# A kernel of polysketch attention and a SiLU layer: every engine's order fixed by a plan, four column tiles in turn, first chunk transposed by PE

## The chip, the cores and the metric

One core of one Trainium2 chip. The metric is the device time of one execution in microseconds (us), as the median of several executions. The kernel before takes 137.73 us (3 executions, 137.29 to 138.01). The span of a profile runs from the first recorded instruction to the last. It is about 1.8 us shorter than the time of the same execution (135.7 against 137.52 for the kernel before).

In the profile, PE is TensorE, PEld its weight loads, DVE is VectorE, ACT is ScalarE, POOL is GpSimd and SP is SyncE. "L239" is a line of the kernel that ran. The chain of waits is followed back from the last instruction. Its lines give start, length, engine, tile and line; "x16" means 16 records run together.

## The reference, cut to what matters

```python
batch, n_heads, seq, head_dim, r = 4, 4, 1088, 32, 8
def phi(x):                       # 64 products of two 8-wide sketches
    a = einsum('rd,bhsd->bhsr', S1, x);  b = einsum('rd,bhsd->bhsr', S2, x)
    return einsum('bhsi,bhsj->bhsij', a, b).reshape(..., 64)
q_p, k_p = phi(q), phi(k)
kv = einsum('bhsf,bhsd->bhfd', k_p, v);  z = sum(k_p, axis=2)
attn = einsum('bhsf,bhfd->bhsd', q_p, kv) / (einsum('bhsf,bhf->bhs', q_p, z) + 1e-6)
x = attn.transpose(0, 2, 1, 3).reshape(4352, 128)
h = x @ w_in                      # 128 -> 2048
out = (h * sigmoid(h)) @ w_out    # SiLU, 2048 -> 128
```

There are four chunks (one for each batch entry) of 1088 rows. In the kernel each chunk gives two blocks of 512 rows for the layer, and the last 64 rows of all four chunks make a ninth block of 256. A block of 512 rows needs eight SiLUs of 128x1024 elements, so there are 64 big ones, and eight half ones for the ninth block.

## The kernel before

Projections run in float32 on 128x32 column tiles of PE (`tile_position`). The pool allocator and the order of the program text decide what each engine does next. The parts that matter here (cuts marked):

```python
def project(srcT, weights):              # keys: 2 weights, queries: 3
    ...
    for c in range(4):
        for i, w in enumerate(weights):  # A, B (, WM) one after the other in tile c
            dst = pa[32*c: 32*(c+1), i, :] if i < 2 else pb[32*c: 32*(c+1), 0:256]
            nc.tensor.matmul(dst, w, srcT[:, c, 0:256], start=True, stop=True,
                             tile_position=(0, 32 * c))
    for c in range(4):
        for i, w in enumerate(weights):  # the 32 columns that are left
            nc.tensor.matmul(...)
    ... # DVE transposes back

def k_side(b):
    nc.vector.transpose(out=KT..., in_=Kx[b]...)    # waits for the load of K
    ab = project(KT, [A, B])
    ... # outer products kp on DVE, key sums z (PE), WM (DVE), kv (PE), KV (DVE)

def q_side(b):
    ... # transposes, project(QT, [A, B, WM]), row scalars, three outer products qp
        nc.sync.dma_start_transpose(qt, qp...)      # then num on PE, copy to xT on ACT

def attn(b):
    if b + 1 < B:
        load_x(Kx, k, b + 1, "Kx"); load_v(b + 1); load_x(Qx, q, b + 1, "Qx")
    k_side(b); q_side(b)

attn(0)
for b in range(B):
    if b + 1 < B: attn(b + 1)
    for g in range(2): moe(xT[b][:, g, :], 512, store_main(b, g))
moe(xR..., B * XN, store_rest)                     # the ninth block, eight stores on one queue
```

The names in the traces: KT and QT are the transposed keys and queries, kp and qp their outer products, z the key sums and kv the sums of kp times v. WAB holds the weights of both sketches, and WM, made from z, those of the denominator. num is qp times kv, which gives xT, the input of the layer; qt is qp transposed. h is the layer's first product, g its SiLU and o the second product. PSUM is the memory that PE writes to, in banks. The prediction calls the layer MoE.

## Time and profile before

| what | us | view |
|---|---|---|
| first SiLU starts | 36.8 | timeline of ACT |
| 64 big and 8 half SiLUs, start to end | 36.8 to 128.5 | the same |
| after the last SiLU | 7.2 | chain of waits, span |
| busy share PE / ACT / DVE | 72% / 53% / 42% | first part of the page |

The page of the kernel before: busy time and share of each engine, then groups of instructions (operation, count, busy time, mean ns, idle time just before them and what ended it).

```profile
PE 97.1 (72%) x773; PEld 48.2 (35%) x784; DVE 56.9 (42%) x128; ACT 72.1 (53%) x90; POOL 15.4 (11%) x35
...
L239 ACT ACTIVATE g<-h_ps 128x1024 bf16<-128x1024 f32 (+1 forms) x72 | 65.6, 986 | 22.2 <-PE h_ps L237 10.6
...
L140 PE MATMUL pa<-KT_131,WAB 128*32 128x256 f32 x32 | 3.0, 509 | 15.6 <-DVE WAB L118 15.6
...
L158 DVE STREAM_TRANSPOSE KT_132<-Kx 128x1024 f32<-128x1024 f32 x2 | 2.5, 1240 | 5.1 <-DMA Kx<-in_k_dram 5.1
```

No engine is full over the whole span, so the shares alone say little. The idle times point to the start: PE stood 15.6 us until the weights (WAB) were on chip, although DVE had only a few small copies to make for them. The chain of waits of the kernel before tells why:

```profile
5.21 8.43 DMA Kx<-in_k_dram
...
13.66 0.04 DVE KT_132 L158
...
15.32 0.18 DVE WAB L118
...
15.63 2.01 PE pa L140 x16
...
31.80 3.18 DMA qt<-qp
```

DVE had the transpose of the second chunk's keys ahead of the WAB copies, and waited for that load until 13.66 us. The whole first chunk then went through before the first SiLU at 36.8 us. Once SiLUs run, PE's work for the next chunk interrupts them. This is the chain of waits of the kernel before in the warm stretch, where one chunk's key projections and sums, and later its query projections, are on PE:

```profile
60.45 1.01 PE pa L140 x16
61.46 0.15 PE pb L144 x14
61.61 0.97 PE h_ps L237 x4
62.58 0.80 PE z_ps L172 x18
...
66.70 1.01 PE pa L140 x6
...
69.50 0.52 PE pb L144 x6
70.11 1.03 ACT g L239
```

A pair of layer matmuls of 512 columns takes 0.43 us when nothing is in its way, so the four at 61.61 would take 0.86 and took 0.11 more. Both key sets together cost PE 1.01 + 0.15 + 0.11 = 1.27 us. The three query sets cost about 3.1 us (66.7 to 69.85), and ACT then waited for PE.

### The profile page before, as it was taken

The page shows a single profiled execution, that of the slowest core. Times are in us where ns is not written, and L with a number is a line of the kernel's source. Part 1 is how long each engine was busy: PE and PEld are TensorE (multiplying, and loading weights), DVE is VectorE, ACT ScalarE, POOL GpSimd, SP SyncE. Part 2 cuts the span into 40 slices and gives each one's busy share as a digit, 9 for nine tenths or more (in the row PEclk, how much of TensorE's full clock was granted, in tenths as well). Part 3 has the DMA queues.
Part 4 walks back from the last instruction along what each step waited for, and adds up shares of the span by engine and source line. Part 5 has one row for each costly group of instructions (what it writes and reads, how often), then busy time and mean ns, then how long its engine had stood idle before and what let it go on. Part 6 is the DMA issues. An engine that isn't in the chain of part 4 may idle for free.

```text
span 135.7 us, 2047 instructions
## 1 busy us (share of the span) xinstructions
PE 97.1 (72%) x773; PEld 48.2 (35%) x784; DVE 56.9 (42%) x128; ACT 72.1 (53%) x90; POOL 15.4 (11%) x35
## 2 busy tenths in 40 slices
PE   0000369500799997999999699999979999998800
PEld 0000256200255643335654234456333334345500
DVE  1250987893058489028269300944950020202010
ACT  0300000000557078988536995461979999998800
POOL 6990001700000900000000000000000000000000
PEclk9999999965589999999999999999999999999975
DMA  4999999906200612824000761220066131130411
GB/s 112 295 180 283 355 252 296 101 5 131 42 0 5 76 6 39 174 39 77 5 0 5 129 107 17 34 44 5 0 127 107 17 56 21 27 55 0 77 22 19
DMA packets 34569, 11.34 MB, mean 84 GB/s; under 512 B 31360, under 2 KB 33408, under 8 KB 34560
## 3 DMA queue, kind: packets, MB, share of 16 engines
q1 hardware_dynamic: 28800, 9.05, 28.9%
q0 software_dynamic: 5664, 2.16, 13.8%
q8 instruction: 6, 0.10, 0.3%
q10 hardware_dynamic: 96, 0.01, 0.1%
q14 instruction: 3, 0.02, 0.1%
HBM read 8.79 MB, written 2.23 MB: 81 GB/s over the span
## 4 chain that ended last, share of the span: by engine, by line
PE 55%; DMA 14%; ACT 13%; DVE 9%; issue 4%; ACTq 0%
PE h_ps L237 17%; PE o_ps L243 16%; ACT g L239 13%; DMA Kx<-in_k_dram 9%; PE pa L140 9%; DMA qt<-qp 5%; PE kv_ps L186 3%; PE pb L140 2%; PE pb L144 2%; PE num L225 2%; DVE qp L216 2%; DVE kp L167 2%; PE z_ps L172 2%; DVE proj L149 1%; DVE QT_133 L196 1%
## 5 line engine op out<-in xcount | busy, mean ns | idle before, releaser
L239 ACT ACTIVATE g<-h_ps 128x1024 bf16<-128x1024 f32 (+1 forms) x72 | 65.6, 986 | 22.2 <-PE h_ps L237 10.6
L243 PE MATMUL o_ps<-g,w_out 128*128 128x512 bf16 (+1 forms) x140 | 38.0, 367 | 0.5 <-ACT g L239 0.3
L237 PEld LDWEIGHTS <-w_in 128*128 128x128 bf16 x144 | 12.9, 97 | 20.1 <-issue 11.1
L246 DVE STREAM_TRANSPOSE ot<-o_ps 128x512 f32<-128x512 f32 (+1 forms) x9 | 6.1, 681 | 32.1 <-PE o_ps L243 26.9
L243 PEld LDWEIGHTS <-w_out 128*128 128x128 bf16 x144 | 13.6, 97 | 15.8 <-issue 2.7
L149 DVE STREAM_TRANSPOSE proj<-pa 128x256 f32<-128x256 f32 x16 | 6.2, 429 | 25.3 <-PE pa L140 18.4
L140 PE MATMUL pa<-KT_131,WAB 128*32 128x256 f32 x32 | 3.0, 509 | 15.6 <-DVE WAB L118 15.6
L77 POOL DMA_DIRECT2D Vb<-in_v_dram x16 | 8.7, 554 | 31.5 <-PE kv_ps L186 29.6
L225 PE MATMUL num<-qt,KV 128*64 128x512 bf16 (+1 forms) x24 | 4.4, 381 | 9.6 <-DMA qt<-qp 9.4
L216 DVE TENSOR_TENSOR qp<-aqs,proj 128x1024 bf16<-128x1024 f32 (+1 forms) x12 | 10.8, 954 | 0.1
L167 DVE TENSOR_TENSOR kp<-proj 128x1280 bf16<-128x1280 f32 (+1 forms) x8 | 10.3, 1332 | 0.0
L237 PE MATMUL h_ps<-xT_141,w_in 128*128 128x512 bf16 x29 | 9.2, 380 | 1.5 <-ACT g L239 1.0
L237 PE MATMUL h_ps<-xT_139,w_in 128*128 128x512 bf16 x30 | 9.0, 387 | 1.4 <-ACT g L239 0.7
L237 PE MATMUL h_ps<-xT_142,w_in 128*128 128x512 bf16 x32 | 9.5, 377 | 0.6 <-ACT g L239 0.5
L237 PE MATMUL h_ps<-xT_140,w_in 128*128 128x512 bf16 x30 | 9.0, 380 | 1.1 <-ACT g L239 0.7
L229 ACT ACTIVATE xT_139<-num 128x512 bf16<-128x512 f32 x2 | 1.2, 597 | 15.1 <-PE num L225 15.1
L175 ACT ACTIVATE zt<-z_ps 32x32 f32<-32x32 f32 x4 | 0.7, 176 | 15.2 <-PE z_ps L172 15.2
L140 PEld LDWEIGHTS pa<-KT_131,WAB 128*32 128x32 f32 x32 | 1.2, 134 | 16.5 <-issue 16.0
L225 PEld LDWEIGHTS <-KV 128*64 128x64 bf16 x24 | 1.4, 112 | 13.9 <-issue 11.1
L140 PE MATMUL pa<-QT_134,WAB 128*32 128x256 f32 x32 | 4.9, 385 | 0.0
L158 DVE STREAM_TRANSPOSE KT_132<-Kx 128x1024 f32<-128x1024 f32 x2 | 2.5, 1240 | 5.1 <-DMA Kx<-in_k_dram 5.1
L172 PE MATMUL z_ps<-proj 128*32 128x32 f32 (+1 forms) x72 | 3.9, 209 | 0.8 <-DVE proj L149 0.8
(70 smaller groups left out, 95.5 us busy)
## 6 DMA issues: line engine op xcount, KB each, us to landing
Kx<-in_k_dram SPq DMA_DIRECT2D x4, 544.0 KB, 6.1
Qx<-in_q_dram SPq DMA_DIRECT2D x4, 544.0 KB, 5.3
out_dram<-ot SPq DMA_DIRECT2D x32, 64.0 KB, 2.0
Vb<-in_v_dram POOLq DMA_DIRECT2D x16, 64.0 KB, 4.4
w_in<-in_moe_w_in_dram POOLq DMA_DIRECT2D x1, 512.0 KB, 8.8
w_out<-in_moe_w_out_dram POOLq DMA_DIRECT2D x1, 512.0 KB, 18.5
qt<-qp SPq DMA_TRANSPOSE x12, 3.2
Vx<-in_v_dram POOLq DMA_DIRECT2D x8, 8.0 KB, 3.1
```

The source lines that it names most:

```text
L77: nc.gpsimd.dma_start(t[32 * c: 32 * (c + 1)].rearrange("p h a d -> p h (a d)"), AP(tensor=v.tensor, offset=v[b, 0].offset + c * NB * D, a ...
L140: nc.tensor.matmul(dst, w, srcT[:, c, 0:256], start=True, stop=True, tile_position=(0, 32 * c))
L149: nc.vector.transpose(out=o[:, i, 0:NB, :].rearrange("p a r -> p (a r)"), in_=pa[:, i, :])
L167: nc.vector.tensor_tensor(out=kp[:, H * lo: H * hi], in0=_bc(a, 2, R), in1=_bc(bb, 1, R), op=ALU.mult)
L172: nc.tensor.matmul(z_ps[:HR, 0:HR], ab[:n, 1, t, :], ab[:n, 0, t, :], start=(t == 0), stop=(t == NB))
L186: nc.tensor.matmul(kv_ps[:, 64 * hp: 64 * (hp + 1)], kpf[:n, t, 128 * hp: 128 * (hp + 1)], vv, start=(t == 0), stop=(t == NB))
L216: nc.vector.tensor_tensor(out=qp, in0=_bc(aqs[:, H * lo: H * hi], 2, R), in1=_bc(bq[:, H * lo: H * hi], 1, R), op=ALU.mult)
L225: nc.tensor.matmul(num[64 * hp: 64 * (hp + 1), :n], KV[:, hp].rearrange("p h d -> p (h d)"), rhs, start=True, stop=True, tile_position=(0, ...
L237: nc.tensor.matmul(h_ps[:, jj, :n], w_in[:, j * P: (j + 1) * P], x, start=True, stop=True)
L239: nc.scalar.activation(out=g[:, :, :n], in_=h_ps[:, :, :n], func=ACT.Silu)
L243: nc.tensor.matmul(o_ps[:, :n], w_out[:, j, :], gs[j // 2][:, j % 2, :n], start=(j == 0), stop=(j == NJ - 1))
L246: nc.vector.transpose(out=ot[:, :n], in_=o_ps[:, :n])
```

## The change: intent and diff

The intent is to start the layer earlier, to make attention cheaper on PE, and to place what is left so that no engine waits. A `Plan` simulates all engines with a guessed cost of each task, sorts by due times, and fixes every engine's order. Projections and key sums run "four column tiles in turn". The first chunk's first half goes through eight PE transposes and two copies on ACT instead of a DMA transpose. The last stores go out on three queues. The core of the diff (cuts marked):

```diff
+class Plan:                       # greedy: the earliest possible task; a due one may go ahead of it
+    def run(self, stretch=1.3):
+        ...
-        for c in range(4):
-            for i, w in enumerate(weights):
-                nc.tensor.matmul(dst, w, srcT[:, c, 0:256], ..., tile_position=(0, 32 * c))
+    def mm_set(dst, srcT, w, lo, hi):         # one weight, four tiles in turn, 288 columns
+        for c in range(4):
+            nc.tensor.matmul(dst[32*c: 32*(c+1), lo:hi], w, srcT[:, c, lo:hi],
+                             start=True, stop=True, tile_position=(0, 32 * c))
...
+        pr = [pl.add("PE", 0.55, lambda sl, i=i: proj(i, sl), st["kt"], take=pool) for i in range(2)]
...
+            if pe:                            # chunk 0, first half
+                e = pl.add("PE", 0.4, ... pet(lo, hi, f, sl), [o], take="o")
+                c.append(pl.add("ACT", 0.55, ... petc(lo, hi, f), [e] + c, give=e))
+            else:
+                c = [pl.add("SP", 1.3 if n > 1 else 0.7, ... dmat(lo, hi), [o], lag=2.2)]
...
+    key_tasks(0, pool="h")
+    query_tasks(0, [(0, 4)], pool="h", pe=True, at=5.3)
+    query_tasks(0, [(4, 8), (8, 9)], at=6.0)  # its second half comes later
+    for b in range(1, B):
+        load(b); key_tasks(b); query_tasks(b, [(0, 4), (4, 8), (8, 9)])
```

## The prediction

> **What bounds it now.** Three stretches (timeline, chain of waits).
> (1) 0 to 36.8 us: no SiLU runs. The window table shows ScalarE 1.5 us busy in 0 to 17. The page's groups show PE idle 15.6 us until the WAB copies: VectorE ran in program order, stood 5.1 us at chunk 1's key transpose until its load landed (13.66), and the WAB copies, needed by chunk 0's first matmul, were queued behind it. Then chunk 0 goes through whole: projection 15.6, outer products until 31.8, DMA transpose 3.2, num, first h at 36.1.
> (2) 36.8 to 128.5: MoE, 91.7 us. Where undisturbed the period is 0.915 us per 1024-wide SiLU; PE needs about 0.87 (four 512-column matmuls), so both engines are nearly full. 64 x 0.915 + 8 half ones (4.0) = 62.6. Attention of chunks 1 to 3 occupies PE in between, about 7.4 us each, read at 60.4 to 69.7: key projection 1.3, key sums 0.85, L2 0.3, kv 0.95, query projection 3.1, num 0.9. That makes 22. About 7 us are stalls (3.25 for one DMA transpose at 76; a cold PE at 36 to 38.5).
> (3) 128.5 to 135.7: last o, transpose, eight stores issued one after another by one queue.
>
> **What the change does.**
> - Start. WAB before everything that waits for a load, chunk 1 loads last. K0 lands about 5.5 (before: 5.2), KT 6.9, keys projected cold about 8; on VectorE then transposes 1.1, kp 1.45, half-sized query work 2, qp 1.22: about 13.4. Eight PE transposes and two 0.6 copies replace the 3.2 us DMA. KV must wait for kp's second half (1.2) and two more query transposes, so it is ready about 15.8; num, copy, h: first SiLU at 17.7, 19 us earlier.
> - Column tiles. Before, consecutive matmuls often hit the same column tile. The Trainium skill ("TensorEngine Tiling (Array Packing)", Key Properties) says different tiles execute in parallel. The trace agrees: 16 key records of 256 columns took 1.09 us at 60.4, about 1.7 if serial (estimate, 256/512 of the 0.216 us pace). Four tiles in turn should give 0.5 for keys, 0.75 for queries, 0.35 for sums: 3.6 us less per chunk, 11 us in all. PE is the path while attention interrupts the MoE, so nearly all counts.
> - Order. Later DMA transposes are planned early enough; I expect one stall of 1 to 3 us near 18 to 22 (chunk 1's keys lie behind both weights on one queue) and 1 to 2 near 30, where chunk 0's second half comes back.
> - Clock. 16 same records took 1.95 us at 22.4 against 1.09 at 60.4. "TensorE: Matmul & The Clock Gate", Part 1, calls this a half-rate clock until PE has been busy some 3.4 us. The first MoE pairs will be cold again: about 2 us lost.
> - End. Eight stores on three queues: about 2 us less.
>
> **Sum.** 17.7 + 62.6 + 3 x 3.75 (attention left on PE) + 1.2 (second half of chunk 0) + 5.5 stalls = 98.2; tail 4.8; span 103, plus 1.8 (run minus span before): 104.5 us. Range 99 to 110. Faster 0.97, same 0.02, slower 0.01.
>
> **Shows it right or wrong.** First SiLU between 16 and 20; PE key projection records at a third to a half of their time in the warm stretch; ScalarE busy share near 70%; SiLU period 0.92 outside attention; no DMA transpose in the chain over 1 us; tail under 5.5.
>
> **What would make it wrong.** The weights or chunk 1 landing after 20 us, since seven loads now share the start; tiles that don't overlap (+8); fixed order making one late item hold an engine; VectorE late for chunk 0's second half (+4); PE cold for longer.

## The result, and the profile after

The kernel after takes **115.99 us** (median of 4; 115.12 to 117.98). Its ratio to the kernel before is 0.8416, with a 95% interval of 0.834 to 0.8491. Ratios here are the mean time of one kernel's runs over that of the other's of the same rounds, so they are not quite the ratio of the medians. The direction was right, but the time lies 6 us above the upper end of the range.

The page of the kernel after, first part:

```profile
PE 93.7 (82%) x647; PEld 39.9 (35%) x657; DVE 59.3 (52%) x117; ACT 73.7 (65%) x93; POOL 16.0 (14%) x38
```

PE is busy for 93.7 us, only 3.4 us less than before, where the prediction had counted on 11 less from the column tiles. That is the first sign of where the miss lies. The span, laid beside the prediction's sum (span 103.05, measured 113.7):

| term | predicted | measured | how it was measured | off |
|---|---|---|---|---|
| first SiLU | 17.7 | 20.58 | timeline of ACT | +2.9 |
| to the end of the stalls: the first 12 SiLUs, chunk 1's attention | 12 x 0.915 + 10.45 = 21.4 | 21.57 | 20.58 to 42.15 | +0.1 |
| the other 52 SiLUs, attention of chunks 2 and 3 | 47.6 + 7.5 = 55.1 | 60.3 | 42.15 to 102.43 | +5.2 |
| 8 half SiLUs | 4.0 | 5.6 | 102.43 to 108.03 | +1.6 |
| after the last SiLU | 4.8 | 5.7 | 108.03 to 113.7 | +0.9 |

The 10.45 are chunk 1's attention (3.75), chunk 0's second half (1.2) and the stalls allowed for (5.5). The 47.6 is 52 x 0.915.

The start, in the chain of waits of the kernel after. Compare it with the 15.63 and 31.80 of before:

```profile
1.32 3.58 DMA Kx<-in_k_dram
...
4.92 0.79 DVE KT_88 L241
...
13.73 1.22 DVE qp L369
14.95 1.15 DVE kp L258
...
16.15 0.95 PE A_145 L289 x8
...
17.78 0.57 PE H_141 L400
```

The second chunk's load no longer stands in the way, and the DMA transpose is gone from this part. The kv sums (L289, eight records of 64 columns) take 0.95 us, and 0.72 where the clock is full (the run e11_warm below).

The stall before chunk 0's second half, same view:

```profile
22.43 2.63 DVE kp L258 x2
25.05 1.16 DVE QT_91 L337
...
26.34 1.10 DVE qp L369
...
27.47 5.43 DMA qt<-qp
...
32.94 0.41 PE A_144 L400 x2
...
35.77 0.26 PE A_145 L400
36.04 0.98 PE H_140 L459 x2
...
37.10 1.03 ACT G_148 L463
```

The outer product of chunk 0's second half (qp at 26.34) was planned for 21.34. On DVE it came after chunk 1's key products (kp) and query transpose (QT_91). Its DMA transpose took 5.4 us; those of before took 3.2 (median). Then PE stood in front of the small num of the last 64 columns (35.77), which nobody needs before the ninth block, with the layer's next pair (36.04) behind it. That num waited for a second, small transpose, which took 6.9 us (DMA view, issued at 29 to 31 us). PE had stood idle for 1.32 us before the big num and 1.89 us before the small one, and the pair then ran at half the clock (0.98 us; 0.54 behind another small num, at 60.01, with a granted clock of 1.00, where it was 0.50 at 36 to 38 us). In the plan the first h stood at 15.41 (19.5 in the trace), and the second half's big num at 26.39 (32.94).

The warm stretch, same view (compare 60.45 to 61.61 of before):

```profile
66.25 0.43 PE H_140 L459 x2
66.69 0.62 PE A_145 L204 x8
67.31 0.54 PE H_141 L459 x2
...
70.73 0.44 PE A_145 L265 x18
```

One set (four matmuls, eight records) costs 0.62 us and 0.11 on the pair after it: 0.73 us. A chunk has five: 3.65 us. With the sums (0.44 + 0.11), the L2 product (0.14), kv (0.95), two num (0.45 each) and the small one (0.26) that makes 6.45 us of PE for a chunk. The prediction had 3.75. The difference, 2.7 us for each of chunks 2 and 3, is the 5.2 of the table within 0.2 us. PE was the path there: from 42.15 to 87.05 us it was busy for 44.36 of 44.90 us (window table).

The end, same view. The half SiLUs took 5.6 us:

```profile
106.71 0.38 PE O_142 L470 x2
107.09 0.23 PE H_141 L459 x2
...
107.41 0.61 ACT G_151 L463
...
108.06 0.39 PE O_142 L470 x2
```

In the ninth block the plan put the o matmuls ahead of the next h, so that ACT waits for o (0.38) and h (0.23) before every second SiLU. In the kernel before, seven of them ran without a gap in 3.97 us.

### The profile page after: what moved, and what is told of

Read it like the earlier page. It is cut to its first block, busy times and chain, and to the rows that moved or that the text cites. A ratio compares the mean times of both kernels' runs of the same rounds, so it can differ in the third digit from the quotient of the medians.

```text
span 113.7 us, 1788 instructions
## 1 busy us (share of the span) xinstructions
PE 93.7 (82%) x647; PEld 39.9 (35%) x657; DVE 59.3 (52%) x117; ACT 73.7 (65%) x93; POOL 16.0 (14%) x38
## 4 chain that ended last, share of the span: by engine, by line
PE 54%; ACT 16%; DVE 14%; DMA 8%; issue 3%; POOL 1%; POOLq 0%; SPq 0%; ACTq 0%
PE H_141 L459 10%; PE O_143 L470 9%; PE H_140 L459 9%; PE O_142 L470 8%; DMA qt<-qp 5%; PE A_145 L204 4%; DVE kp L258 3%; PE A_144 L204 3%; DMA Kx<-in_k_dram 3%; ACT G_148 L463 3%; DVE qp L369 3%; ACT G_149 L463 3%; ACT G_147 L463 3%; ACT G_150 L463 3%; PE A_145 L289 2%
## 5 line engine op out<-in xcount | busy, mean ns | idle before, releaser
L459 PEld LDWEIGHTS <-w_in 128*128 128x128 bf16 x144 | 12.4, 102 | 18.5 <-issue 11.1
L463 ACT ACTIVATE G_146<-H_140 128x1024 bf16<-128x1024 f32 (+1 forms) x12 | 12.0, 1000 | 3.1 <-PE A_144 L204 2.1
L463 ACT ACTIVATE G_151<-H_141 128x1024 bf16<-128x1024 f32 (+1 forms) x12 | 11.6, 965 | 3.4 <-PE H_141 L459 2.6
L463 ACT ACTIVATE G_148<-H_140 128x1024 bf16<-128x1024 f32 (+1 forms) x12 | 12.0, 996 | 2.5 <-PE H_140 L459 2.3
L463 ACT ACTIVATE G_147<-H_141 128x1024 bf16<-128x1024 f32 (+1 forms) x12 | 12.0, 996 | 2.1 <-PE H_141 L459 2.1
L463 ACT ACTIVATE G_149<-H_141 128x1024 bf16<-128x1024 f32 (+1 forms) x12 | 12.0, 999 | 1.5 <-PE H_141 L459 1.4
L463 ACT ACTIVATE G_150<-H_140 128x1024 bf16<-128x1024 f32 (+1 forms) x12 | 11.5, 959 | 2.1 <-PE A_145 L204 1.3
L446 POOL DMA_DIRECT2D out_dram<-ot x2 | 1.1, 560 | 80.2 <-DVE ot L475 80.2
L369 DVE TENSOR_TENSOR qp<-aqs,qabm 128x1024 bf16<-128x1024 f32 (+1 forms) x12 | 11.1, 939 | 0.1
L258 DVE TENSOR_TENSOR kp<-kab 128x1280 bf16<-128x1280 f32 (+1 forms) x8 | 10.6, 1350 | 0.1
L475 DVE STREAM_TRANSPOSE ot<-O_143 128x512 f32<-128x512 f32 x4 | 2.9, 718 | 13.7 <-PE O_143 L470 13.7
L475 DVE STREAM_TRANSPOSE ot<-O_142 128x512 f32<-128x512 f32 (+1 forms) x5 | 3.3, 664 | 12.7 <-PE O_142 L470 12.5
L253 DVE STREAM_TRANSPOSE kab<-A_145 128x288 f32<-128x288 f32 x3 | 1.4, 480 | 9.3 <-PE A_145 L204 9.3
L459 PE MATMUL H_140<-xT_135,w_in 128*128 128x512 bf16 x15 | 5.6, 457 | 0.3 <-ACT G_148 L463 0.3
L459 PE MATMUL H_141<-xT_135,w_in 128*128 128x512 bf16 x15 | 5.3, 433 | 0.2 <-issue 0.2
L459 PE MATMUL H_141<-xT_138,w_in 128*128 128x512 bf16 x16 | 4.8, 379 | 0.3 <-ACT G_151 L463 0.2
L459 PE MATMUL H_141<-xT_137,w_in 128*128 128x512 bf16 x16 | 4.8, 383 | 0.0
L459 PE MATMUL H_140<-xT_137,w_in 128*128 128x512 bf16 x15 | 4.6, 381 | 0.1
L459 PE MATMUL H_141<-xT_136,w_in 128*128 128x512 bf16 x15 | 4.6, 382 | 0.0
L289 PEld LDWEIGHTS <-kp 128*128 128x128 bf16 (+1 forms) x72 | 3.7, 103 | 2.1 <-issue 0.4
```

The source lines that it names most:

```text
L253: nc.vector.transpose(out=st["ab"][:, i].rearrange("p a r -> p (a r)"), in_=st[f"p{i}"][:, 0:CW])
L258: nc.vector.tensor_tensor(out=st["kp"][:, H * lo: H * hi], in0=_bc(a, 2, R), in1=_bc(bb, 1, R), op=ALU.mult)
L289: nc.tensor.matmul(st["kvp"][:, 64 * hp: 64 * (hp + 1)], kpf[:n, t, 128 * hp: 128 * (hp + 1)], Vb[b][:n, 2 * hp: 2 * hp + 2, t, :], start= ...
L369: nc.vector.tensor_tensor(out=qp, in0=_bc(st["aqs"][:, H * lo: H * hi], 2, R), in1=_bc(bq, 1, R), op=ALU.mult)
L446: eng[2 * r + c].dma_start(AP(tensor=out.tensor, offset=out[4 * NB + c, 32 * r].offset, ap=[[SA * DM, 32], [S * DM, B], [1, 32]]), o[32 * ...
L459: nc.tensor.matmul(cc[jp][:, jj, :n], w_in[:, j * P: (j + 1) * P], x, start=True, stop=True)
```

## The experiments

Each kernel is the kernel after with one edit. "Moves" are made on the plan's finished order, so that nothing else is planned anew, unless said otherwise. All results were correct.

### What a projection set costs

**e1_double.** Every set is issued twice.

```diff
-        for c in range(4):
+        for c in 2 * list(range(4)):
```

> Every projection set (four 288-column fp32 matmuls in four column tiles) is issued twice in a row into the same bank; the result stays right. Measure: in the stretch with a full clock (after 42 us), the time from the start of the matmul pair before a set to the start of the pair after it, less the 0.43 us of a pair. In the changed kernel that is 0.72 us. Theory D (the tiles do overlap; 0.24 us is streaming[...], and some 0.48 us is entering and leaving the column-tiled mode): 0.96 us. Rival S (the tiles overlap badly, the 0.72 us is the work itself): 1.2 to 1.4 us. Whole kernel: D about +4 to +5 us, S about +9 to +12 us.

Measured: 121.21 us (one execution). From the chain of waits:

```profile
69.84 1.18 PE A L204 x16
71.02 0.54 PE H L459 x2
```

Two sets cost 1.18 + 0.11 = 1.29 us here (and 1.22 at most other places of the same chain, where the record is 1.11). So the second set adds about 0.49 to 0.56, and about 0.24 is paid once. D's 0.96 failed. The cost of the two sets lies in S's range (1.2 to 1.4), but the kernel became 5.2 us longer, near D's 4 to 5. S's reading, that the tiles overlap badly, is settled by e17 and e18 below: they overlap fully, and one set is longer work than D took it for.

**e2_adjacent.** Each tile's 288 columns in two halves, both halves of a tile in a row, so that neighbours in the order hit the same tile.

```diff
+        mid = (lo + hi) // 2
         for c in range(4):
-            nc.tensor.matmul(dst[.., lo:hi], w, srcT[:, c, lo:hi], ...)
+            for l, u in ((lo, mid), (mid, hi)):
+                nc.tensor.matmul(dst[.., l:u], w, srcT[:, c, l:u], ...)
```

> Each tile's 288 columns are cut in two halves that are issued one after the other before the next tile's turn, as consecutive matmuls met the same tile in the kernel before. Same columns in all. Same measure as for e1_double (0.72 us in the changed kernel). Theory D (tiles overlap only with other tiles): five serial slots of 0.12 us instead of two, 0.60 + 0.48 = 1.08 us per set. Rival S (no useful overlap anyway): stays near 0.72 to 0.8 us.

Measured: 113.61 us (one execution); a set cost 0.74 us instead of 0.72 to 0.73, the number of rival S and not D's 1.08. Two neighbours on the same tile do no harm, which contradicts the ground on which the prediction expected a gain from taking the tiles in turn. Why the whole kernel was 2 us shorter was not followed up: only one execution was taken, and its trace differs from that of after mainly in the length of the stall.

**e17_same_tile and e18_two_tiles.** Each full set is followed by four more of the same matmul, all in tile 3, or in tiles 2 and 3.

```diff
-        for c in range(4):
+        for c in (0, 1, 2, 3) + ((3, 3, 3, 3) if hi - lo == CW else ()):   # e17
+        for c in (0, 1, 2, 3) + ((2, 3, 2, 3) if hi - lo == CW else ()):   # e18
```

> The after kernel, in which each full set (four 288-column matmuls in tiles 0 to 3) is followed by four more of the same matmul, all in tile 3 (same result). In e1_double four more in tiles 0 to 3 cost 0.49 us. Theory P2 (a float32 matmul streams its columns twice, 0.24 us for 288 columns on one tile at the 512-column pace of 0.216 us, and tiles overlap two at a time): the four more cost 0.96 us. Theory P4 (a float32 matmul takes four times its columns, 0.49 us on one tile, and four tiles do overlap fully): they cost 1.9 to 2.0 us. Theory P1 (the same rate on one tile as on four, no overlap at all): 0.49 us. Read in the warm stretch from the chain, set and following pair, not from the kernel's time (which should be 5 to 20 us longer than after).

> As e17_same_tile, with the four more in tiles 2, 3, 2, 3. P2 (two at a time is all there is): 0.49 us for the four more, as in e1_double. P4 (overlap grows with the number of tiles): 0.95 to 1.0 us. P1: 0.49 us.

Measured in the warm stretch: 143.94 and 128.15 us in all. Chain of waits of e17_same_tile:

```profile
65.28 2.56 PE A L204 x16
67.84 0.54 PE O L470 x2
```

and of e18_two_tiles:

```profile
63.26 1.59 PE A L204 x16
64.86 0.54 PE H L459 x2
```

The four more cost 2.56 - 0.62 = 1.94 us in one tile, 1.59 - 0.62 = 0.97 in two, and 0.49 in four (e1_double, e9_grouped). P4 is right and P1 and P2 are wrong. (Only the time of the whole kernel missed: e17 is 28 us longer than after, not 5 to 20.) A float32 matmul of 288 columns takes 1.94 / 4 = 0.485 us in its tile. That is four times its columns at the pace of the bf16 matmuls (0.216 us for 512). And four tiles do overlap fully. So 0.49 us is what a set costs with perfect overlap. The four extra matmuls of e17 also write the same columns of the same bank one after another. So does the second set of e1_double, at 0.49, but a version of e17 with separate columns was not run.

With this the sets of before can be judged (estimates from these numbers): eight matmuls of 288 columns, one by one, would take 8 x 0.485 = 3.9 us, and perfect overlap 0.97. They took 1.27, of which about 0.24 is the fixed part if it was the same there. The keys of before were then already within 0.1 us of perfect overlap, so there was nothing to win. The queries of before, with three matmuls in a row in each tile, took about 3.1 where perfect overlap takes 1.46. Why they overlapped less than the keys is not shown: e2 had two in a row, and no run had three.

**e9_grouped.** The two key sets are one task, and so are the three query sets (from chunk 0's second half on); the plan is made anew.

```diff
-        pr = [pl.add("PE", 0.55, lambda sl, i=i: proj(i, sl), st["kt"], take=pool) for i in range(2)]
+        pr = pl.add("PE", 1.2, proj, st["kt"], take=pool, need=2)       # both sets, two banks
...
+            pr = [pl.add("PE", 0.24 + 0.165 * nn, set3, [t, kst["wm"]], take=pool, need=need)]
```

> Projection sets are issued together: both key sets in one go, all three query sets in one go (from chunk 0's second half on), so the column-tiled mode is entered and left twice per chunk instead of five times; same columns. After e1 and e2 I put a set at 0.48 us of streaming plus 0.24 us of changing mode. Theory: the key group costs 1.20 us of PE (start of pair before to start of pair after, less 0.43) instead of 2 x 0.72, the query group 1.68 instead of 3 x 0.72: 0.7 us less per chunk, 2 us in all, if the plan's other moves do no harm (it makes a new order). Rival 1, no cost of changing mode (0.72 all streaming): 1.44 and 2.16. Rival 2, mode change 0.48 as in theory D: 0.96 and 1.2.

Measured: 111.66 us, ratio 0.8111 (0.8042 to 0.818). Chain of waits:

```profile
62.44 1.11 PE A L209 x16
63.55 0.54 PE H L502 x2
...
68.22 1.60 PE A L367 x32
69.82 0.54 PE O L513 x2
```

One, two and three sets cost 0.73, 1.22 and 1.71 us: 0.49 each and 0.24 once. That a part is paid once for each group is shown. That it is the change of tiling is a reading: 0.11 of it lies in the pair that follows, and the kv sums, which use no column tiles, leave the same 0.11 behind them (a pair of 0.54 at 82.94 us of after). The kernel's gain is not all due to it, as the stall at 27 to 37 us also changed with the new plan.

### The stall before chunk 0's second half

**e3_rest_late.** Moves the num and copy of chunk 0's last 64 columns to just before the next use of their PSUM bank.

```diff
+        nxt = next(e for e in order[at + 1:] if e[0]["take"] == "att" and e[0]["slot"] == m["slot"])
+        ... # m8 and x8 of chunk 0 are taken out and put in front of nxt
```

> In the changed kernel PE and ScalarE stood at chunk 0's last 64 columns (num from the second, small DMA transpose, 35.8 us) although nothing needs them before the end, with the h of the second half behind them in order. Here this num and its copy come just before the next use of their PSUM bank; nothing else moves. Theory order: the first h of the second half starts right after its copy, about 34.0 instead of 36.0 us, one cold pair less: 2 to 3 us less than the changed kernel (ratio to before about 0.82 to 0.827 against 0.842). Rival (another wait ends at the same time, as the outer products or key transposes of the next chunk on VectorE): under 0.7 us less.

Measured: 111.47 us, ratio 0.8123 (0.8066 to 0.8179). Chain of waits:

```profile
26.80 5.14 DMA qt<-qp
...
33.09 0.60 PE H L463 x2
...
33.77 1.03 ACT G L467
```

The layer's pair starts at 33.09 instead of 36.04, at the full clock, and five SiLUs follow without a gap. A small num at the wrong place of a fixed order cost some 4 us.

**e4_loads_late.** Moves chunk 3's loads (POOL) behind chunk 0's second half, held by a one-column copy on POOL that reads it.

```diff
+        order[at:at] = [(dict(fn=lambda: nc.gpsimd.tensor_copy(out=gate, in_=xT[0][:, 1, 0:1])), ())] + mine
```

> Chunk 3's loads (K, V, Q) wait, by a one-column copy on GpSimd, until chunk 0's second half is copied to xT; in the changed kernel they run from 20 to 35 us, over the DMA transposes of 27.5 us, of which the first landed after 5.4 us against 3.1 in the median. Theory contention: that transpose lands in about 3.2 us, PE's wait before num shrinks by 2 us and the small one follows, 2 to 4 us less in all. Rival (the transpose is slow for another reason, for instance two transposes issued together, or chunk 2's loads): it still takes over 4.5 us, time within 1 us of the changed kernel.

Measured: 111.84 us, ratio 0.8127 (0.8086 to 0.8168). The time gained what was expected, but not by the way that was expected. From issue to landing (DMA view), the big transpose of the second half took 4.6 us here and 5.4 in after, where 3.2 (the median of all twelve before) had been expected, and over 4.5 by the rival. The small one of the last 64 columns took 3.6 instead of 6.9, so that its num ran at 32.61 instead of 35.77. Hardly anything else moved at that time. The next big transpose, which now runs under the moved loads, took 5.21 us. So moving the loads took 0.8 us off the big transpose and 3.3 off the small one, the one that PE had stood for; why the big one still takes 4.6 stays unexplained.

**e5_both.** Both moves together.

> e3_rest_late and e4_loads_late together. They gave 0.8123 and 0.8127 of the kernel before, 0.029 less than the changed kernel each. Theory: both cure the same stall (PE and ScalarE waiting for chunk 0's second half, and the cold PE after it), so they do not add: 0.803 to 0.812. Rival, independent stalls: 0.78 to 0.79.

Measured: 112.44 us, ratio 0.817 (0.8105 to 0.8235). The gains do not add, as the theory said, though the ratio lies above its range too: both moves remove the same wait for the small num. What is left is the wait for the big transpose, 5.03 us in the chain even with the loads moved away, and the next one, now under the moved loads, took 4.89.

**e6_pe_second.** e3_rest_late, and chunk 0's second half goes through eight PE transposes and two ACT copies instead of the DMA.

```diff
+    def pet2():
+        for t in range(8):
+            nc.tensor.transpose(pt[:, t, :], qf[:, t, :], identb)
+        for f in range(2):
+            nc.scalar.activation(out=qt[:, 4*f: 4*f + 4], in_=pt[:, 4*f: 4*f + 4], func=ACT.Copy)
```

> e3_rest_late with chunk 0's second half transposed on PE (eight transposes, two copies of 0.6 us on ScalarE) instead of by the DMA, all other instructions in the same order. Theory: the DMA transpose's 5 us is the last wait there; without it the first h of the second half starts at 31.5 to 32.3 us instead of 33.1 in e3_rest_late, PE does not stand over 0.8 us before it, and the kernel is 0.5 to 1.5 us faster than e3_rest_late (ratio 0.80 to 0.809). Rival: the copies delay SiLU by what they save; equal to e3_rest_late within 0.5 us.

Measured: 110.99 us, ratio 0.8078 (0.7997 to 0.8158). The second half's first SiLU comes at 32.97 instead of 33.77, and the kernel gains 0.5 us, within the intervals of e3. The wait for the DMA is gone. The chain now runs through DVE's list until 24.25 us (chunk 1's kp), and from 24.30 through PE's own list, almost without a gap, to the num at 31.25.

**e8_dma_first.** Undoes one part of the change: chunk 0's first half by DMA transpose, planned anew.

```diff
-    query_tasks(0, [(0, 4)], pool="h", pe=True, at=5.3)
+    query_tasks(0, [(0, 4)], pool="h", at=5.3)
```

> One part of the change undone: chunk 0's first half goes through the DMA transpose again (the plan then makes its own order; qp is ready at 15 us, loads of chunk 1 and 2 are in flight). PE transposes took from 15.0 to 16.7 us and KV was only ready at 17.4, so PE transposes cannot have won more than the DMA's time beyond 17.4. If the DMA transpose takes 3.4 us as in the quiet kernel before, the first SiLU comes 1 to 1.5 us later than 20.6; if it takes over 5 us as under loads, 3 to 4 us later. I expect the second: first SiLU at 23.5 to 24.5, kernel 2 to 4 us slower than the changed one.

Measured: 114.21 us, ratio 0.8271 (0.8178 to 0.8363). The first SiLU came at 24.70, close to what was expected (its DMA transpose took 6.47 us), but the kernel was not slower than after: it was some 2 us faster, with intervals that just overlap (after: 0.834 to 0.8491). The expectation that an early start is worth its time was wrong: in after, ACT stands still later, because the second half is not ready, and in e8 it hardly does (the gap before it, at 36.47, is 1.25 us). The 4 us that the PE transposes gain at the start were given back in the stall.

**e12_measured.** The plan gets eighteen costs as the trace of after showed them (a set 0.7, kv 0.95, a transpose's lag 2.6 to 3.6, and so on), with the grouped sets of e9 and the last block's order of e10; planned anew. Chunk 0's second half still goes through the DMA transpose.

```diff
-            pl.add("PE", 0.15 + 0.045 * nn, lambda sl, i=i: proj(i, sl), ...)
+            pl.add("PE", 0.7, lambda sl, i=i: proj(i, sl), ...)
... # seventeen more of this kind
```

> e9_grouped with the half order of e10, and the plan's costs replaced by those measured in the changed kernel's trace (outer products 0.3 per block, projections 0.7, kv 0.95, query scalars 1.0 + 0.12 per block, the first DMA transposes 4.9 us with issue). Theory (the stall came from a plan whose clock runs ahead of the chip): chunk 0's qp of the second half is now before chunk 1's key work on VectorE, PE does not stand over 1 us between 25 and 40 us, and the kernel takes 106 to 109 us (ratio 0.77 to 0.79). Rival (order is not what was wrong): 110 us or more.

Measured: 117.8 us, ratio 0.85 (0.8438 to 0.8561), 6 us slower than e9_grouped, the same kernel without the new costs and the half order, and no faster than after (the intervals overlap). A miss. Chunk 0's second half did come early (its rows at 30.67). But the first SiLU slipped to 21.22, and later chunks arrive with nothing in hand. PE in the timeline of e12_measured, with idle time before a group in brackets:

```profile
84.75 0.59 PE L514 MATMUL O<-G,w_out 128*128 128x512 bf16 x2 [0.31 <-ACT G L507]
87.25 0.41 PE L432 MATMUL A<-qt,KV 128*64 128x512 bf16 x2 [1.91 <-DMA qt<-qp]
88.34 1.61 PE L503 MATMUL H<-xT,w_in 128*128 128x512 bf16 x4 [0.69 <-ACT xT L440]
```

PE runs dry for chunk 3's transpose and then works at half the clock (1.61 us for four matmuls that otherwise take 0.86). Better costs alone did not make a better plan. A likely reason, argued and not tested, is that a greedy plan that brings each chunk just in time has no slack when a transpose takes 3.2 us instead of the planned 2.6. Which of the eighteen costs did the harm was not separated.

### The cold clock at the start

**e11_warm.** Idle PE at the start is filled with matmuls of zeros into a free bank: nine before the first work, five behind chunk 0's first kv part.

```diff
+    def dummies(n):
+        for _ in range(n):
+            nc.tensor.matmul(bank("o", 1), dum[:, 0:P], dum[:, P:], start=True, stop=True)
+    dummies(9)
```

> Nine matmuls of zeros before chunk 0's first work and five in PE's idle time at 12.5 us keep PE busy; nothing else moves. Theory clock: the records of chunk 0 then run at full clock (a first h pair in 0.6 us instead of 1.0, num 0.41 instead of 0.63, kv's second half unchanged), and the first SiLU starts at 18.3 to 19.3 us instead of 20.6; kernel 1 to 2 us faster, if the later stall does not take it back. Rival (the start is set by VectorE, loads and hops, not by PE's clock): first SiLU within 0.5 us of 20.6.

Measured: 113.94 us, ratio 0.8248 (0.8197 to 0.83). The first SiLU came at 18.38 instead of 20.58: kv 0.72 us, the first h pair 0.60. The cold clock is worth 2.2 us of the 2.9 that the start was late. The stall before the second half grew meanwhile (its two DMA transposes took 6.6 and 7.1 us), and its first SiLU came at 35.47, against 37.10 in after.

### The order in the last block

**e10_half_order.** In the ninth block, each h goes ahead of the o of two before it.

```diff
+        for jp in range(NJ // 2 - 2):
+            ... # move h[jp + 2] in front of o[jp]
```

> One thing moved: in the last, half-wide block each h pair comes before the o pair that the plan had put in front of it (as the scheduler of the kernel before had it). In the changed kernel the eight half SiLUs took 5.6 us (102.43 to 108.03), two in 1.34 us, with o waiting for the newest SiLU in front of the next h; in the kernel before 4.0 us. Theory: 4.0 to 4.3 us again, 1.3 to 1.6 us less for the kernel. Rival (another wait sets the pace): under 0.5 us.

Measured: 114.05 us, ratio 0.8231 (0.8181 to 0.828). ACT in the timeline of e10_half_order:

```profile
98.97 3.56 ACT L468 ACTIVATE G<-H 128x1024 bf16<-128x1024 f32 x4
102.86 3.97 ACT L468 ACTIVATE G<-H 128x512 bf16<-128x512 f32 x7 [0.32 <-PE H L464]
```

Seven half SiLUs again run in 3.97 us, as in the kernel before. The span of the profile fell from 113.7 to 112.6.

### Together

**e13_combo.** e6_pe_second and e10_half_order.

> e6_pe_second plus the half order of e10, the plan's list otherwise untouched. If both gains are separate: 1.3 to 1.6 us less than e6_pe_second, 109.2 to 109.8 us (ratio 0.795 to 0.80).

Measured: 110.67 us, ratio 0.8003 (0.7955 to 0.805). That is less than e10 alone, but the interval overlaps that of e6 alone (0.7997 to 0.8158): of the 1.3 to 1.6 us expected on top of e6, the ratios show about 1 us, the medians 0.3.

**e14_combo_warm.** e13_combo with the dummies of e11_warm.

> e13_combo (110.67 us, ratio 0.8003) with the dummy matmuls of e11_warm at the start, nothing else moved. Theory A (the stall before chunk 0's second half was what took back the gain of the warm start in e11; e13 has hardly a stall there, so the gain now arrives at the end): first SiLU about 18.3 us (e13: near 20.4), second half of chunk 0 starts its SiLUs 1 to 2 us earlier than e13's 33.3 us, and the kernel takes 108.5 to 109.3 us, ratio 0.785 to 0.791. Rival B (between 22 and 33 us VectorE's list for chunk 1 and 0 sets when the second half is ready, whatever happens before): first SiLU 18.3 us too, but the second half's first SiLU within 0.5 us of 33.3 and the kernel at 110 to 110.7 us, ratio 0.796 to 0.801.

Measured: **109.77 us**, ratio 0.7918 (0.7884 to 0.7952), the fastest of all. But the test is not clean. The first SiLU was expected at 18.3 and came at 19.57. ScalarE in the timeline of e14_combo_warm:

```profile
17.38 0.60 ACT L417 ACTIVATE xT<-H 128x512 bf16<-128x512 f32 x1 [1.70 <-PE H L409]
19.57 1.02 ACT L474 ACTIVATE G<-H 128x1024 bf16<-128x1024 f32 x1 [1.59 <-PE H L470]
```

In this profile the clock fell in spite of the dummies: the window table has a granted clock of 0.79 at 15 to 17 us and 0.50 at 17 to 19, and the first h pair took 1.03 us. So only 0.4 us was gained at the start here, and 0.57 at the second half (32.72 against 33.29). The ratio is 0.0085 below that of e13, about 1.2 us of the time before, and their intervals just fail to touch. Even that leans on two of the six executions (110.38 and 110.86) left out as slow, being over 1.5% above the fastest. Whether a start that stays warm would pass on its full 2 us stays open. Theory A's first step did not happen, and B was not tested.

**e15_combo_grouped and e16_grouped_warm.** e9_grouped with the three other parts of e13_combo, without and with the dummies.

> e9_grouped (projection sets of a chunk issued one after the other, so PE changes its tiling fewer times) with the three other parts of e13_combo (chunk 0's last 64 columns late, its second half by PE transposes, h in front of o in the last block). If a change of tiling costs 0.24 us of PE and two less per 5 sets are saved for keys and queries together 0.24 + 2 x 0.24 = 0.7 us per chunk in the PE-bound stretch (chunks 2 and 3, and part of chunk 1): 1.4 to 2 us under e13, 108.6 to 109.3 us, ratio 0.786 to 0.791. Rival: the grouped sets hold two banks of PSUM and PE for 1.7 us at a time, in which ACT runs dry (it has at most one h ready), so that nothing is gained: 110 to 112 us, ratio 0.798 to 0.813.

> e15_combo_grouped with the dummy matmuls of e14. If both theories A and the 0.24 us of each change hold, the two gains add, as the one falls before 33 us and the other after it: about 107 to 108 us, ratio 0.775 to 0.782. If the early gain is taken back before the second half, the same as e15 within 0.5 us.

Measured: 112.56 us, ratio 0.8127 (0.8093 to 0.8161), and 111.82 us, ratio 0.8081 (0.8051 to 0.8111). The rival was right about the time: grouping is slower than e13_combo, although each group saves PE 0.24 us per set joined. Chunk 1's first half reaches xT at 42.26 us in e15 and at 37.83 in e13. WM is not what held its query sets back: it is there at 27.3 us in e15 and 26.9 in e13, but the sets start at 31.88 in e15 and at 27.39 in e13. The group needs two PSUM banks at once, as the rival said, but the plan's order is another too, and e15's first layer pairs and key group still ran at half pace (the key group's records take 1.96 us at 21.7; those of e13, at 19.8, take 1.18). Which of these cost the time was not separated. e16 gained 0.7 us over e15, with intervals that overlap and nothing like the sum expected: its first SiLU came 1.24 us earlier (19.71 against 20.95), its third only 0.23 (24.00 against 24.23).

## Why the prediction was wrong, point by point

**The failed step: "Four tiles in turn should give 0.5 for keys, 0.75 for queries, 0.35 for sums: 3.6 us less per chunk".** Measured: 1.46 for keys (two sets of 0.73; before 1.27), 2.19 for queries (before about 3.1), 0.55 for sums. Attention left on PE is 6.45 us per chunk, not 3.75. This accounts for 5.2 of the 10.65 us by which the span was off. The prediction's own check failed in the same place: the key records were to fall to a third or a half, and took 2 x 0.62 = 1.24 us against 1.16 before. The error behind it is in the sentence "about 1.7 if serial (estimate, 256/512 of the 0.216 us pace)". It gave each of the 16 records, two for each matmul, the column pace of bf16 matmuls, and so each float32 matmul twice that pace. e17 shows four times: 0.485 us for 288 columns in one tile. Serial would have been 3.9 us for the key sets. The 1.27 us of before was not weak overlap with much left to win: it was nearly full overlap.

The prediction cited the Trainium skill, "TensorEngine Tiling (Array Packing)", Key Properties, that different tiles execute in parallel. That is right, and e1, e18 and e17 show it cleanly: 0.49, 0.97 and 1.94 us for the same four matmuls in four, two and one tile. What the prediction took from it, that the kernel before did not have it yet, was wrong for keys and half right for queries. The same section says that changing the tiling mode drains TensorE. The trace is in line with that (0.24 us paid once for each group of sets, e9, though no run shows that all of it is the drain), and the prediction left such a cost out: the change makes five trips into the column tiles per chunk for its projections where the kernel before made two.

**Start, "first SiLU at 17.7".** 20.58. The mechanism was right: WAB early, the second chunk's load out of the way, PE transposes for the DMA, 16 us gained of the 19 predicted. The term was mis-sized by 2.9 us. e11 shows 2.2 of it to be the clock. The prediction named the cold clock, but only for the first key projections and the layer's pairs, not for kv, num and the later projections before them. The Trainium skill ("TensorE: Matmul & The Clock Gate", Part 1) calls the window free-running and the count of cold matmuls variable from run to run; e11 (warm) and e14 (cold again with the same dummies) are in line with that, with one profile each.

**"One stall of 1 to 3 us near 18 to 22 and 1 to 2 near 30", "VectorE late for chunk 0's second half (+4)".** The sum was right within 0.1 us, the place was not. It was one long stall, from 31 to 37 us, and two of its causes were named: DVE came to qp 5 us later than planned, and a fixed order let one late item hold PE (the small num, 4 us by e3). Not foreseen was that the DMA transposes would take 5.4 us (big) and 6.9 us (small), of which 0.8 and 3.3 went away with the load traffic in e4. It cost as much as the smaller stalls allowed for, which is luck and not insight, the more so as the same row of the table holds chunk 1's attention, forecast at 3.75 us like the two others.

**"8 half ones (4.0)".** 5.6. The prediction carried the rate of before over and did not look at the new order of h and o in the last block, which the comparison of the orders would have shown. e10 gives it back.

**Tail, "4.8".** 5.7 us instead of 7.2 before: right in kind, 0.9 short. No experiment was made on it.

**"No DMA transpose in the chain over 1 us", "ScalarE busy share near 70%".** Both failed (5.43 us; 65%), and both point at the same stall and the same PE time. The SiLU period outside attention held (0.90 to 0.92 us for the SiLUs that start from 87.05 to 90.68; 0.92 forecast).

So the large change moved the time by 21.7 us. What was missing lay half in a gain that the kernel before already had, and half in waits that a fixed order made and that three small moves (e3, e6, e10) took away: 115.99 to 110.67 us.

## What to carry to other kernels

Before counting on overlap, measure what one such instruction costs alone, in its own data type; without that number, "already overlapped" and "serial" look the same in a trace. In a fixed order look for the items that nobody needs soon, and put them where a late arrival holds up nobody: one small matmul cost 4 us here, and corrected costs in the planner did not help. Time gained at the start counts only if the next piece of work comes earlier too (e8: the 4 us gained were all given back).

## What the Trainium skill lacked or had wrong

- "TensorEngine Tiling (Array Packing)", Theoretical Speedup, says up to 4x for 32-column tiles. The runs agree for float32: 1.94 us in one tile, 0.97 in two, 0.49 in four (e17, e18, e1). This page has no cost of a float32 column. The skill as a whole does not lack it: "FP8 and Floating Point Precision", TensorE Precision Notes, gives true float32 four passes through the array, which the prediction did not use. The runs agree: a float32 column costs four times a bf16 one, 0.485 us for 288 columns against 0.216 us for 512.
- The same page, Key Properties, says that a change of tiling mode drains TensorE and gives no number. Here each group of sets in column tiles paid 0.24 us once (one, two and three sets: 0.73, 1.22, 1.71 us, e9). That is at most what a way in and out costs, as 0.11 of it also follows the kv sums, which use no column tiles.
- "TensorE: Matmul & The Clock Gate", Part 1, describes a half rate, and these runs agree: after the stall, pairs took 0.85 us (39.19 and 40.04 us of after), and 0.43 soon afterwards. None of them shows what keeps the clock up for certain: with the same nine and five dummies it stayed up in e11 and was lost at about 16 us in e14. Also, the profile's granted clock read 1.00 at 15 to 20 us of after, while its records were slower than in the warm e11 (num 0.64 us against 0.41, a set of 160 columns 0.76 against 0.48): the records decide.
- None of the pages cited here has the latency of a DMA transpose beside other traffic: a median of 3.2 us from issue to landing in the kernel before; 5.4 (big) and 6.9 (small) beside the loads in after at 27 to 33 us; 4.6 and 3.6 where those loads were moved away in e4, 5.0 and 4.0 in e5.
